# Quarter-array products for the odd groups, K^T V of two batches moved behind such products, K and V fetched ahead of Q, and the copies of the last column halves exchanged

## The chip, the cores and the metric

The kernel runs on one core of a Trainium2 chip. The metric is the device time of one execution in microseconds (us), lower is better. TensorE (PE in the profile, with its weight loads as PEld), VectorE (DVE), ScalarE (ACT) and GpSimd (POOL) compute; SyncE (SP), ScalarE and GpSimd issue transfers (DMA).

## The reference

For 8 batches, 8 heads, 576 rows and a head dimension of 64, attention without softmax, a normalisation for each head and row, and a feed-forward layer:

```python
kv = np.einsum('bhsd,bhse->bhde', k, v)
out = np.einsum('bhsd,bhde->bhse', q, kv)
rms = np.sqrt(np.mean(out * out, axis=-1, keepdims=True) + 1e-06)
out = out / rms * g_norm
x = out.transpose(0, 2, 1, 3).reshape(4608, 512)
h = x @ w_in                                    # 512 x 2048
g = np.where(h > 0.0, h, np.exp(np.minimum(h, 0.0)) - 1.0)
result = g @ w_out                              # 2048 x 512
```

The matrix products take bf16 operands and sum in float32.

## The kernel before

**Tokens.** A batch has 576 rows, held as 9 slots of 64. The 72 slots are taken eight at a time, so there are nine groups of 512 tokens (T = 0 to 8); `slot_of(T, n)` gives the batch and the slot. Since 9 is odd, each odd group (1, 3, 5, 7) has one pair of slots whose halves belong to two batches; in the even groups every pair is of one batch.

**Feed-forward.** A group's first product is eight steps `M0` to `M7`, each eight matmuls of 128x512 into a pair of PSUM banks (L381, `mm1_part`), followed by exp on ScalarE (L349) and two operations on VectorE that finish the elu (L361, L365; steps `E0` to `E7`). The second product is eight half-steps `H0` to `H7` of eight matmuls each (L402, `mm2_half`), whose results ScalarE copies out (L418).

**Attention of a group from 2 on.** `se_mm` (L240) multiplies the turned Q of two slots (128 tokens) by K^T V of their batch, for each of eight heads: contraction over 64, output 64 wide. Where both slots are of one batch, one matmul takes half of the array (64 rows, 128 columns; the profile writes 64\*128) and gives 128 tokens. Where they are of two batches, two matmuls take a quarter each (64\*64). A group is two calls, `se0` and `se1`. ScalarE squares (L276), VectorE sums (L282), ScalarE takes Ln and Exp (L290, L291), VectorE scales (L298), four DMA transposes turn the result (L305), VectorE multiplies by the gain (L311, steps `G0`, `G1`).

**K^T V of a batch** is `kv_all` (L257): 72 matmuls in quarters of the array (L155), 64x64 each, into a PSUM pair, and one copy by ScalarE (L261).

**The order** is written out by hand and no scheduler changes it. For each T from 2 to 8 `window` (L760) walks a string of steps: the first product of group T (M, E), the second of group T-1 (H), the attention of group T+1 (X: both products, squares, sums, inverse roots; Y: scale and transposes), and Q: turn Q of batch T+2 by DMA transposes on SP's queue (`turn_q`, L330), let GpSimd wait for them (`after_turn`, L338), and fetch batch T+3 (`fetch_ahead`, L92) by three transfers on GpSimd's queue: Q in float32, then K and V as bf16. GpSimd casts Q of batch T+2 at the start of window T (`cast_q`, L103). The letter after a step names its PSUM pair: A, B and C are one pair of banks each, and `o_ps` has the two banks left. Each is free again when its last reader is through. Window 2 has a string of its own, with `XB` in it; windows 3 to 7 go

```python
kv = f"K{T + 1}C" if T + 1 < B else ""
steps = (
    f"M0B {kv} H1 E0 M1A H3 E1 M2B H4 E2 H5 XA Y H6 Q M3B H7 E3 M4A E4 M5C E5 M6B G0 E6 M7A G1 E7 h0 h2"
)
```

so that K^T V of batches 4 to 7 stands in windows 3 to 6, between M0 and H1. The last 128 rows of the output are made in two halves of 256 columns (`last_columns`, L433): 16 matmuls of 128x256 each (L439), a copy (L110 on ScalarE, L112 on VectorE), and two transfers to memory, issued by ScalarE and SP (`last_store`, L426).

Of the kernel before, what the change touches and what calls it, by code (L numbers as in the profile page):

```python
# [8 lines left out]
FP32 = mybir.dt.float32  # L9
# [7 lines left out]
def kernel(  # L17
# [14 lines left out]
    P = 128  # L32

    B, H, S, D = q.shape
    DM = H * D
    DF = moe_w_in.shape[1]
    RK = S // 64
# [5 lines left out]
    V, A, Q = nc.vector, nc.scalar, nc.gpsimd  # L43

    const = ctx.enter_context(tc.tile_pool(name="const", bufs=1))
    stage = ctx.enter_context(tc.tile_pool(name="stage", bufs=1))
# [28 lines left out]
    def slot_of(T, n):  # L75
        return divmod(8 * T + n, RK)

    bf, raw = {}, {}
    src_of = {"q": q, "k": k, "v": v}

    def fetch(name, b, u=None):

        if (name, b) not in bf:
            bf[name, b] = qkvp.tile([P, 4, RK, D], BF16, name=f"{name}_bf", tag=name)
        ms = slice(0, 4) if u is None else slice(u, 4, 2)
        load(bf[name, b][:, ms], name, b, ms)

    def load(dst, name, b, ms=slice(0, 4), eng=nc.gpsimd):
        in_ = src_of[name][b].rearrange("h r d -> (h r d)").rearrange("(m p x) -> p m x", m=4, p=P)
        eng.dma_start(out=dst.rearrange("p m j d -> p m (j d)"), in_=in_[:, ms, :])  # L90

    def fetch_ahead(b):  # L92
        raw[b] = stage.tile([P, 4, RK, D], FP32, name="st_q", tag="q")
        load(raw[b], "q", b)
        for name in "kv":
            fetch(name, b)

    def cast_q(b):

# [67 lines left out]
    def kv_of(b, l, u, s):  # L167
        return kv_sb[l * 64 : l * 64 + 64, b, u, s]
# [46 lines left out]
    class Turned:  # L215
# [7 lines left out]
        def product(self, y):  # L223
            self.y = y
            y_mm(self.T, self.u, y)
# [11 lines left out]
        def scale(self, l):  # L237
            scale_t(self.T, self.y[l], self.r[:, l, :], 2 * l + self.u)

    def se_mm(T, h, se_ps):  # L240

        for i in range(2):
            (b0, j0), (b1, j1) = (slot_of(T, 4 * h + 2 * i + t) for t in range(2))
            parts = [(0, P, b0, j0, 2)] if b0 == b1 else [(0, 64, b0, j0, 1), (64, P, b1, j1, 1)]
            for m in range(4):
                u, s = m // 2, m % 2
                for l in range(2):
                    for lo, hi, b, j, n in parts:
                        nc.tensor.matmul(  # L249
                            se_ps[lo:hi, l, (4 * i + m) * 64 : (4 * i + m) * 64 + 64],  # L250
                            lhsT=qT[b][l * 64 : l * 64 + 64, s, u, j : j + n, :],
                            rhs=kv_of(b, l, u, s),
                            start=True,
                            stop=True,
                        )

    def kv_all(b, tag):  # L257
        kv_ps = pair(tag, "kv_ps")
        for u in range(2):
            kv_mm(b, [kv_ps[:, s, :] for s in range(2)], u)  # L260
        return lambda: nc.scalar.copy(  # L261
            kv_sb[:, b], kv_ps[:, :, 0:P].rearrange("p s (u e) -> p u s e", u=2)
        )

    def attention(T):

        st = {}

        def se(h):
            def product(tag="C"):  # L270
                st["se", h] = pair(tag, "se_ps")
                se_mm(T, h, st["se", h])

            def square():
                sq = attp.tile([P, 2, DM], BF16, name="sq", tag="sq")
                nc.scalar.activation(sq, st["se", h], AF.Square)  # L276
                st["sq", h] = sq

            def sums():
                ss = attp.tile([P, 2 * H], FP32, name="ss", tag="ss")  # L280
                st["ss", h] = ss
                nc.vector.reduce_sum(  # L282
                    out=ss,
                    in_=st.pop(("sq", h)).rearrange("p l (m e) -> p (l m) e", e=D),
                    axis=AX.X,
                )

            def inv():
                ss = st["ss", h]
                nc.scalar.activation(ss, ss, AF.Ln, bias=eps_col, scale=1.0 / D)  # L290
                nc.scalar.activation(ss, ss, AF.Exp, scale=-0.5)  # L291

            def scale():
                if h == 0:
                    st["xs"] = attp.tile([P, J, DM], BF16, name="xs", tag="xs")
                    x_tile(T)
                se_ps, ss = st.pop(("se", h)), st.pop(("ss", h))
                nc.vector.tensor_tensor(  # L298
                    out=st["xs"][:, 2 * h : 2 * h + 2, :].rearrange("p i (l m e) -> p l i m e", l=2, e=D),
                    in0=se_ps.rearrange("p l (i m e) -> p l i m e", i=2, e=D),  # L300
                    in1=ss.rearrange("p (l i m) -> p l i m", l=2, i=2).unsqueeze(4).to_broadcast([P, 2, 2, 4, D]),
                    op=ALU.mult,
                )
                for i in (2 * h, 2 * h + 1):
                    nc.sync.dma_start_transpose(  # L305
                        out=xT[T][:, :, i * P : i * P + P], in_=st["xs"][:, i, :]
                    )

            def gain():
                cols = slice(2 * h * P, 2 * h * P + 2 * P)  # L310
                nc.vector.tensor_scalar(  # L311
                    out=xT[T][:, :, cols],
                    in0=xT[T][:, :, cols],
                    scalar1=g_col,
                    scalar2=None,
                    op0=ALU.mult,
                )

            return product, square, sums, inv, scale, gain

        pieces = {}
        for h in range(2):
            for name, piece in zip(("se", "sq", "sum", "inv", "mul", "gain"), se(h)):
                pieces[f"{name}{h}"] = piece
        return pieces
# [106 lines left out]

    def last_columns():  # L433

        for n, eng in enumerate((A, V)):
            cols = slice(n * 256, n * 256 + 256)
            ps = single("m", "o_ps")[:, 0:256]
            for f in range(FC):
                nc.tensor.matmul(  # L439
                    ps,  # L440
                    lhsT=gT[NT - 1][:, f, (J - 1) * P : J * P],
                    rhs=w_out_sb[:, f, cols],
                    start=(f == 0),
                    stop=(f == FC - 1),
                )
            o = outp.tile([P, 2, DM], FP32, name="o_sb", tag="o")[:, 0, 0:256]
            copy_on(eng, o, ps)
            last_store(J - 1, o, cols)
# [93 lines left out]
    y_ps, sq0 = {}, {}  # L542
# [123 lines left out]
    for u in range(2):  # L666
        n = Turned(1, u)
# [92 lines left out]
    def window(T, steps):  # L760

        rest = {}
        nxt = attention(T + 1) if T + 1 < NT else None
        for step in steps.split():
            kind, arg = step[0], step[1:]
            if kind in "MR":  # L770
                i, tag = int(arg[0]), arg[1]
                make = mm1_rest if T == 2 and i == 0 else mm1
                rest[i] = make(T, i, tag, kind == "R")
            elif kind == "E":
                rest.pop(int(arg))()
            elif kind == "H":
                mm2_half(T - 1, int(arg))
            elif kind == "h":
                mm2_half(T, int(arg))
            elif kind == "K":  # L780
                kv_all(int(arg[0]), arg[1])()
            elif kind == "X":
                nxt["se0"](arg)
                nxt["se1"]("C")
                for name in ("sq0", "sq1", "sum0", "sum1", "inv0", "inv1"):
                    nxt[name]()
            elif step == "Y":
                nxt["mul0"]()
                nxt["mul1"]()
            elif step == "Q":  # L790
                b = T + 2
                if b < B:
                    turn_q(b)
                if b + 1 < B:
                    after_turn(b)
                    fetch_ahead(b + 1)
            elif kind == "G":
                nxt[f"gain{arg}"]()
            else:
                raise ValueError(step)  # L800
# [4 lines left out]
    for T in range(2, NT):  # L805
        if T + 2 < B:
            cast_q(T + 2)
        if T == 2:
            steps = "M0B K3C E0 M1A H5 E1 M2B E2 R3A H6 E3 XB Y H7 Q M4A E4 h0 R5B E5 M6C G0 E6 M7A G1 E7 h2"
        elif T + 1 < NT:  # L810
            kv = f"K{T + 1}C" if T + 1 < B else ""
            steps = (
                f"M0B {kv} H1 E0 M1A H3 E1 M2B H4 E2 H5 XA Y H6 Q M3B H7 E3 M4A E4 M5C E5 M6B G0 E6 M7A G1 E7 h0 h2"
            )
        else:
            steps = "M0B H1 E0 M1A H3 E1 M2B H4 E2 M3A H5 E3 M4B H6 E4 M5A H7 E5 M6B E6 M7A E7 h0 h2"
        window(T, steps)
# [33 lines left out]
```

## Time and profile before

| | |
|---|---|
| Median of 7 runs (lowest to highest) | 284.14 us (283.87 to 284.18) |
| The profiled execution: its own time | 284.04 us |
| Its span, first to last instruction | 282.3 us |
| PE busy | 273.8 us (97%) |
| DVE, ACT, POOL busy | 163.2, 141.6, 49.5 us |
| Granted TensorE clock | 1.0 |
| DMA | 39.46 MB, mean 140 GB/s |

Busy shares are averages over the whole span. The chain of work that ended last is more telling: it is followed backwards from the last instruction, at each step to what released it, and its pieces lie end to end, so that a piece which becomes shorter shortens the run unless another chain takes over. Matmuls are pipelined: 128x512 matmuls that follow each other start 0.216 us apart, though one lasts 0.38 us. Some records are missing from a trace: in the chain a group of eight such matmuls can appear as seven with a bit of "issue" in the place of the eighth; the distance between the starts of the pieces around it holds what it took.

### The profile page before, as it was taken

The numbers are of one execution on the slowest core, as the hardware profiler recorded it, in microseconds if no ns is written. First come the engines' busy times: TensorE is split into PE (matmuls) and PEld (weight loads), VectorE is DVE, ScalarE is ACT, GpSimd is POOL, SyncE is SP. The second block draws the span as 40 slices with busy tenths as digits, with TensorE's granted clock in tenths as the row PEclk, the third lists the DMA queues.
The fourth block names the chain that finished last, engine by engine and source line by source line (L and its number), as shares of the span: only waits on it lengthen the run. The fifth ranks groups of instructions, "written<-read, shape, count | busy, mean of one in ns | idle before, by whom it ended". The sixth has DMA issues, their size and how long they took to land.

```text
span 282.3 us, 5145 instructions
## 1 busy us (share of the span) xinstructions
PE 273.8 (97%) x2094; PEld 129.6 (46%) x2123; DVE 163.2 (58%) x222; ACT 141.6 (50%) x209; POOL 49.5 (18%) x89
## 2 busy tenths in 40 slices
PE   8899999999999999999999999999999999999994
PEld 3444444444544444444444444444444444444443
DVE  2549532967457746865587448834893489344600
ACT  3778359594566445533552445344543464333321
POOL 7743303322123033033003300000000000000000
PEclk9999999999999999999999999999999999999999
DMA  7999999899999969489438952612160215020222
GB/s 212 192 204 206 207 253 244 176 259 140 186 263 180 155 186 238 94 199 250 113 74 178 268 126 41 149 49 74 40 111 0 77 37 112 0 77 1 74 74 74
DMA packets 50571, 39.46 MB, mean 140 GB/s; under 512 B 30964, under 2 KB 44020, under 8 KB 50548
## 3 DMA queue, kind: packets, MB, share of 16 engines
q0 software_dynamic: 15008, 21.30, 37.7%
q1 hardware_dynamic: 35136, 17.31, 29.1%
q10 hardware_dynamic: 404, 0.53, 0.5%
q8 instruction: 16, 0.26, 0.4%
q14 instruction: 7, 0.06, 0.1%
HBM read 36.70 MB, written 9.44 MB: 163 GB/s over the span
## 4 chain that ended last, share of the span: by engine, by line
PE 95%; DVE 2%; issue 1%; ACT 1%; DVEq 0%
PE h_ps L381 42%; PE o_ps L402 42%; PE kv_ps L155 2%; PE se_ps L249 2%; PE kv_ps L524 2%; PE h_ps L568 1%; PE o_ps L439 1%; PE qt_ps L173 1%; PE mean L198 1%; DVE xT L211 1%; PE y_ps L188 1%; ACT elu_e L349 0%; DVE kv_sb L112 0%; ACT rT L631 0%; DVE qT L112 0%
## 5 line engine op out<-in xcount | busy, mean ns | idle before, releaser
L402 PE MATMUL o_ps<-w_out_sb,gT 128*128 128x512 bf16 x542 | 127.0, 379 | 1.5 <-issue 1.0
L381 PE MATMUL h_ps<-xT,w_in_sb 128*128 128x512 bf16 (+1 forms) x551 | 125.5, 376 | 0.6
L349 ACT ACTIVATE elu_e<-h_ps 128x1024 bf16<-128x1024 f32 (+1 forms) x79 | 74.0, 951 | 72.8 <-PE h_ps L381 71.5
L381 PEld LDWEIGHTS <-w_in_sb 128*128 128x128 bf16 x560 | 54.5, 98 | 64.4 <-issue 0.7
L402 PEld LDWEIGHTS <-gT 128*128 128x128 bf16 x560 | 53.5, 98 | 63.9 <-issue 0.9
L365 DVE TENSOR_TENSOR gT<-elu_e,h_ps 128x1024 bf16<-128x1024 bf16 (+1 forms) x67 | 77.2, 1157 | 6.9 <-DVE elu_e L361 0.5
L361 DVE TENSOR_SCALAR elu_e<-elu_e 128x1024 bf16<-128x1024 bf16 x72 | 31.6, 439 | 59.4 <-ACT elu_e L349 59.3
L418 ACT COPY o_sb<-o_ps 128x512 f32<-128x512 f32 x32 | 18.4, 588 | 31.0 <-PE o_ps L402 31.0
L103 POOL CAST q_bf<-st_q 128x384 bf16<-128x384 f32 x36 | 18.1, 549 | 40.2 <-DMA st_q<-in_q_dram 40.2
L282 DVE TENSOR_REDUCE ss<-sq 128x16 f32<-128x1024 bf16 x14 | 16.5, 1214 | 13.3 <-ACT sq L276 13.3
L298 DVE TENSOR_TENSOR xs<-se_ps,ss 128x1024 bf16<-128x1024 f32 x14 | 16.5, 1215 | 1.2 <-ACT ss L291 1.2
L276 ACT ACTIVATE sq<-se_ps 128x1024 bf16<-128x1024 f32 x14 | 13.7, 1029 | 0.3 <-PE se_ps L249 0.3
L211 DVE SCALAR_TENSOR_TENSOR xT<-y_ps,g_col,rT 128x512 bf16<-128x512 f32 (+1 forms) x10 | 6.2, 639 | 10.1 <-ACT rT L208 7.9
L338 POOL COPY gate<-qT 1x16 bf16<-1x16 bf16 x5 | 1.0, 193 | 55.9 <-DMA qT<-q_bf 55.9
L354 ACT ACTIVATE elu_h<-h_ps 128x1024 bf16<-128x1024 f32 (+1 forms) x12 | 9.3, 816 | 0.0
L90 POOL DMA_DIRECT2D v_bf<-in_v_dram x11 | 7.8, 712 | 4.1 <-DMA w_in_sb<-in_moe_w_in_dram 2.1
L155 PEld LDWEIGHTS <-k_bf 64*64 64x64 bf16 x576 | 6.3, 107 | 5.0 <-issue 4.6
L90 POOL DMA_DIRECT2D k_bf<-in_k_dram x11 | 7.7, 704 | 2.8 <-DMA w_in_sb<-in_moe_w_in_dram 2.1
L155 PE MATMUL kv_ps<-v_bf,k_bf 64*64 64x64 bf16 x576 | 7.5, 194 | 0.6 <-DVE kv_sb L112 0.4
L290 ACT ACTIVATE ss<-ss,eps_col 128x16 f32<-128x16 f32 x14 | 4.3, 308 | 6.4 <-DVE ss L282 6.4
L311 DVE TENSOR_SCALAR xT<-xT,g_col 128x1024 bf16<-128x1024 bf16 x14 | 6.7, 480 | 1.2 <-DMA xT<-xs 1.2
L365 DVE TENSOR_TENSOR gT<-elu_e,elu_h 128x1024 bf16<-128x1024 bf16 x9 | 6.3, 705 | 1.6 <-ACT elu_h L354 1.0
(56 smaller groups left out, 94.1 us busy)
## 6 DMA issues: line engine op xcount, KB each, us to landing
st_q<-in_q_dram POOLq DMA_DIRECT2D x6, 1152.0 KB, 8.2
out_dram<-o_sb SPq DMA_DIRECT2D x24, 256.0 KB, 3.3
k_bf<-in_k_dram POOLq DMA_DIRECT2D x6, 576.0 KB, 10.5
v_bf<-in_v_dram POOLq DMA_DIRECT2D x6, 576.0 KB, 13.0
out_dram<-o_sb SPq DMA_DIRECT2D x19, 128.0 KB, 2.4
w_out_sb<-in_moe_w_out_dram POOLq DMA_DIRECT2D x4, 512.0 KB, 15.6
w_in_sb<-in_moe_w_in_dram POOLq DMA_DIRECT2D x2, 512.0 KB, 10.9
q_bf<-in_q_dram POOLq DMA_DIRECT2D x3, 288.0 KB, 13.4
```

Of the source, the lines that this page charges most:

```text
L90: eng.dma_start(out=dst.rearrange("p m j d -> p m (j d)"), in_=in_[:, ms, :])
L103: nc.gpsimd.tensor_copy(out=bf["q", b][:, u, js], in_=raw[b][:, u::2, js, :].rearrange("p l j d -> p j l d"),)
L155: nc.tensor.matmul(kv_ps[s][l * 64 : l * 64 + 64, u * 64 : u * 64 + 64], lhsT=bf["k", b][rows, 2 * l + u, j, :], rhs=bf["v", b][rows, 2 * ...
L276: nc.scalar.activation(sq, st["se", h], AF.Square)
L282: nc.vector.reduce_sum(out=ss, in_=st.pop(("sq", h)).rearrange("p l (m e) -> p (l m) e", e=D), axis=AX.X,)
L298: nc.vector.tensor_tensor(out=st["xs"][:, 2 * h : 2 * h + 2, :].rearrange("p i (l m e) -> p l i m e", l=2, e=D), in0=se_ps.rearrange("p l ...
L349: nc.scalar.activation(e[:, lo:hi, :], h, AF.Exp)
L361: nc.vector.tensor_scalar(out=e, in0=e, scalar1=1.0, scalar2=1.0, op0=ALU.min, op1=ALU.subtract)
L365: nc.vector.tensor_tensor(out=gT[T][:, 2 * i + lo : 2 * i + hi, :], in0=e[:, lo:hi, :], in1=h, op=ALU.add if relu else ALU.max,)
L381: nc.tensor.matmul((ps[a] if isinstance(ps, list) else ps[:, a, :])[:, cols], lhsT=w_in_sb[:, c, f * P : f * P + P], rhs=xT[T][:, c, cols] ...
L402: nc.tensor.matmul(o_ps[T, j], lhsT=gT[T][:, f, j * P : j * P + P], rhs=w_out_sb[:, f, :], start=(f == 0), stop=(f == FC - 1),)
L418: nc.scalar.copy(o_sb[T, half][:, j % 2, :], o_ps[T, j])
```

## The change

Four parts. First, `se_mm` can make all its products in quarters; the step X asks for it where T is even (that is, for the odd groups 3, 5 and 7) and where K^T V follows (`XA6B` in window 4, for group 5, and `XA7B` in window 5, for group 6). Groups 4 and 8 stay as they were. Second, K^T V of batches 6 and 7 leaves windows 5 and 6 and goes into windows 4 and 5, directly behind `se1`, into the pair B; ScalarE's copy of it then stands between the two squares. Third, from window 3 on the fetch has K and V ahead of Q (batches 6 and 7). Fourth, VectorE copies the first half of the last columns and ScalarE the second.

```diff
-    def fetch_ahead(b):
-        raw[b] = stage.tile([P, 4, RK, D], FP32, name="st_q", tag="q")
-        load(raw[b], "q", b)
-        for name in "kv":
-            fetch(name, b)
+    def fetch_ahead(b, order="qkv"):
+        for name in order:
+            if name == "q":
+                raw[b] = stage.tile([P, 4, RK, D], FP32, name="st_q", tag="q")
+                load(raw[b], "q", b)
+            else:
+                fetch(name, b)
...
-    def se_mm(T, h, se_ps):
+    def se_mm(T, h, se_ps, quarters=False):
...
-            parts = [(0, P, b0, j0, 2)] if b0 == b1 else [(0, 64, b0, j0, 1), (64, P, b1, j1, 1)]
+            parts = [(0, 64, b0, j0, 1), (64, P, b1, j1, 1)]
+            if b0 == b1 and not quarters:
+                parts = [(0, P, b0, j0, 2)]
...
-        for n, eng in enumerate((A, V)):
+        for n, eng in enumerate((V, A)):
...
-                nxt["se0"](arg)
-                nxt["se1"]("C")
-                for name in ("sq0", "sq1", "sum0", "sum1", "inv0", "inv1"):
+                quarters = len(arg) > 1 or T % 2 == 0
+                nxt["se0"](arg[0], quarters)
+                nxt["se1"]("C", quarters)
+                nxt["sq0"]()
+                if len(arg) > 1:
+                    kv_all(int(arg[1]), arg[2])()
+                for name in ("sq1", "sum0", "sum1", "inv0", "inv1"):
                     nxt[name]()
...
-                    fetch_ahead(b + 1)
+                    fetch_ahead(b + 1, "qkv" if T == 2 else "kvq")
...
-            kv = f"K{T + 1}C" if T + 1 < B else ""
+            now = f"K{T + 1}C" if T in (3, 4) else ""
+            behind = f"{T + 2}B" if T in (4, 5) else ""
             steps = (
-                f"M0B {kv} H1 E0 M1A H3 E1 M2B H4 E2 H5 XA Y H6 Q M3B H7 E3 M4A E4 M5C E5 M6B G0 E6 M7A G1 E7 h0 h2"
+                f"M0B {now} H1 E0 M1A H3 E1 M2B H4 E2 H5 XA{behind} Y H6 Q M3B H7 E3 M4A E4 M5C E5 M6B G0 E6 M7A G1 E7 h0 h2"
             )
```

More of the change, by code (lines that the diff above doesn't have):

```diff
@@ L269, in se, with product @@
         def se(h):
-            def product(tag="C"):
+            def product(tag="C", quarters=False):
                 st["se", h] = pair(tag, "se_ps")
-                se_mm(T, h, st["se", h])
+                se_mm(T, h, st["se", h], quarters)
             def square():
```

## The prediction

> **What bounds the kernel now.** I read the page's first and fourth parts, then the chain of waits in order of time, then the timelines of single engines around the places that the diff touches.
>
> ```profile
> PE 273.8 (97%) x2094; PEld 129.6 (46%) x2123; DVE 163.2 (58%) x222; ACT 141.6 (50%) x209; POOL 49.5 (18%) x89
> PE 95%; DVE 2%; issue 1%; ACT 1%; DVEq 0%
> ```
>
> The chain is TensorE's own for 95% of the span: nothing else ends last for long, so what TensorE issues less is won, as long as no other engine becomes late. The chain of windows 4 to 6:
>
> ```profile
> 126.09 0.71 PE kv_ps L155 x72
> 126.79 0.16 issue
> 126.95 1.67 PE o_ps L402 x7
> 128.62 1.73 PE h_ps L381 x8
> ...
> 137.26 0.81 PE se_ps L249 x40
> 138.07 0.32 PE o_ps L402
> 138.39 0.05 issue
> 138.44 1.46 PE o_ps L402 x6
> 139.90 1.73 PE h_ps L381 x8
> ...
> 166.62 0.57 PE se_ps L249 x32
> ...
> 195.73 0.70 PE se_ps L249 x40
> ```
>
> Read the distance between the pieces of big matmuls on either side, less 1.73 us for the eight between (the piece of eight, 1.73, stands in the rows). K^T V costs 128.62 - 126.09 - 1.73 = 0.80, by the unrounded starts 0.81 us. The attention product of group 5 costs 139.90 - 137.26 - 1.73 = 0.91; group 3, worked out in the same way from its rows (82.00 to 84.64), 0.91; group 6 (166.62 to 169.02) 0.67; group 7 (195.73 to 198.27) 0.81; groups 4 and 8 0.68 each. The starts of the windows agree: 124.36, 153.72, 182.84, 212.08 and 240.39 give 29.36, 29.12, 29.24 and 28.31 us for windows 4 to 7; window 7, without K^T V, is 0.81 shorter than window 5, which has it. So an all-half product costs 0.68, and the same with one mixed pair 0.13 (pair at the end, one change of form more) or 0.23 (pair in the middle, two more): some 0.12 us for a change of form, of which the eight extra products are a part.
>
> ```profile
> 127.04 0.37 ACT L261 CAST kv_sb<-kv_ps 128x256 bf16<-128x256 f32 x1
> 135.43 1.22 DVE L365 TENSOR_TENSOR gT<-elu_e,h_ps 128x1024 bf16<-128x1024 bf16 x1
> 137.78 1.95 ACT L276 ACTIVATE sq<-se_ps 128x1024 bf16<-128x1024 f32 x2
> 155.37 0.78 PE L155 MATMUL kv_ps<-v_bf,k_bf 64*64 64x64 bf16 x72
> 276.71 0.37 ACT L110 COPY o_sb<-o_ps 128x256 f32<-128x256 f32 x1 [1.16 <-PE o_ps L439]
> 278.51 0.42 DVE L112 COPY o_sb<-o_ps 128x256 f32<-128x256 f32 x1 [11.10 <-PE o_ps L439]
> ```
>
> The fourth of these gives the price of a quarter product: 72 in 0.78 us, the last lasting 0.19, so (0.78 - 0.19)/71 = 8.3 ns from start to start. Four quarters work side by side.
>
> **The change, part by part.** *Price of a stretch of quarters.* 72 at 8.3 ns are 0.60; K^T V costs 0.81 in all, so entering and leaving the form costs 0.21. 64 products (an attention product in quarters) then cost 0.21 + 0.53 = 0.74, and 64 + 72 in one stretch 0.21 + 1.13 = 1.34 us.
>
> *Group 3 (window 2):* 0.91 becomes 0.74, -0.17. *Group 7 (window 6):* 0.81 becomes 0.74, -0.07. *Group 5 and K^T V of batch 6 (window 4):* 0.91 + 0.81 = 1.72 becomes 1.34, -0.38. *Group 6 and batch 7 (window 5):* 0.67 + 0.81 = 1.48 becomes 1.34, -0.14; here quarters make the product itself dearer by 0.07, and only the shared entry pays. Together -0.76 us.
>
> No trace of before has a stretch of 136 quarters or the passage from `se1` to K^T V. Bounds for that passage: nothing (both are quarters in the same places of the array; inside K^T V the passage from one column block to the other is not seen) and 0.12, a change of form. For a quarter product: 7.9 ns (the first sets of four inside K^T V start 31.6 ns apart) and 9.7 (0.70/72, ends included). I take nothing and 8.3, since rows of the very form give them. The dear ends cost 2 x 0.12 + 4 x 64 x 1.4 ns = 0.60; the cheap one gives 0.10.
>
> The Trainium skill speaks against the part: "TensorE: Matmul & The Clock Gate", section "Wait — 56ns, not 53.3ns?", has starts never closer than about 25 ns, however small the matmul. By it the 104 added products (24 + 24 + 32 + 24) would be 2.6 us, and after the saved switches the run some 1.6 us slower, an estimate from that page. The trace has 8.3 ns for such products in four quarters, so the row decides.
>
> *What the moved K^T V waits for.* It needs pair B, which M2B's elu leaves when DVE's operation at 135.43 ends, at 136.65; in window 4 it starts behind 64 products, near 137.7: 1 us spare. It needs K and V of batch 6 by then. Their transfers:
>
> ```profile
> st_q<-in_q_dram POOLq DMA_DIRECT2D x1, 1152.0 KB, 8.6
> k_bf<-in_k_dram POOLq DMA_DIRECT2D x1, 576.0 KB, 11.1
> v_bf<-in_v_dram POOLq DMA_DIRECT2D x1, 576.0 KB, 13.6
> ```
>
> Issued at 122.68, 123.43 and 124.16, they land at 131.3, 134.5 and 137.8, one behind the other: in the old order V would be there 0.1 us before its use. With K and V first, V lands near 133 and Q last, near 137.8. GpSimd's casts of Q (2.96 us, at 131.38 now) then end near 140.8; behind them on POOL wait the gate at 151.3 and the next fetch. SP turns batch 6 at 147.59, behind the transposes of xs, so 6 us are spare. In window 5 the transfers land by 165.9, K and V near 161, for K^T V near 166.6; the casts end near 169, SP's turn is at 178. The casts move onto DVE's sums and scales; in window 2 they lie there already (85.15 to 87.9) and those took their usual 1.21 us. Cost nothing.
>
> *ScalarE.* The copy (0.37) goes between the squares. Queued behind it are the second square and what hangs on it: DVE's second sum starts 0.2 later (it stands in DVE's queue behind the first sum, which hides the rest), the scales follow 0.2 to 0.35 later, while TensorE's own stretch is longer by 1.34 - 0.91 = 0.43. M4A, which waits for the first scale, has 1.0 us spare now (142.3 against 143.36) and keeps it. M3B, which now waits for the copy: the copy ends near 139.3, M3B starts behind H6 near 140.4. 1.1 us spare; if that cover went, M3B to M7A would start later by what is missing. Transposes and gains keep their 1.6 us before the next M0, for the same reason.
>
> *Windows 5 and 6 without K^T V at their start* are ordered as window 7 is now, and its chain has no wait there. H1's gT has the 16 matmuls of h0 and h2 and M0 as cover.
>
> *The end.* The last copy is on the path. VectorE starts it 0.09 after the last matmul's end and takes 0.42; ScalarE, in the first half, 0.04 and 0.37. That is -0.10; between -0.05 (the durations alone) and -0.15. ScalarE now issues the first half's transfer before that copy (0.50 us, from about 277.2), through at 277.7, well before 278.4. SP's queue keeps its order.
>
> **Sum:** -0.76 - 0.10 = -0.86 us on the profiled execution's 284.04 (span 282.3 and 1.7 around it): 283.18. The median lies 0.10 above that execution, so 283.25, -0.3%. Measurement can tell about 0.2% (0.57 us) from nothing: a limit of 283.57.
>
> **Rivals.** *1. The saving is half as large:* the passage costs a switch, or a long stretch runs at the dear price. Against: the rows of the form. 0.86 - 0.60 gives -0.26, so 283.5 to 283.9. *2. The won time is handed on:* a wait of about 1 us more than its cover in windows 4 and 5 (the copy before M3B, or pair B). For: spare times are only 1.0 to 1.2. Against: each was counted along its queue. Half a us lost twice gives about 284.2. *3. The instruction stream, slower than before.* The long stretch is 136 pairs of weight load and matmul, 272 instructions in 1.13 us; the longest now is 144. The page's instruction queue brought 16 blocks, 0.26 MB, in 0.4% of 16 engines' time, so about 1.1 us for a block of 16 KB. If a block runs out inside each long stretch and the next is a whole 1.1 us away, the two cost 2.2 - 0.86 = +1.3, 285.5; it decides from 0.72 us a stretch. Against: K^T V now eats 144 instructions in 0.6 us with no gap. No row shows how far ahead TensorE holds instructions. "Runtime: NRT & Kernel Launch", section "Instruction fetch mechanics", of the Trainium skill gives TensorE room for 2048 instructions and in another sentence two lines of 256; the first excludes this rival, the second doesn't.
>
> **How the numbers follow.** Forecast (283.0 to 283.45) 0.66; rival 1, 0.14, about a third of it under the limit; rival 2, 0.10, mostly within 0.2%, a fifth slower; rival 3, 0.10. Faster 0.66 + 0.05 = 0.71; slower 0.02 + 0.08 = 0.10, the short stalls of rival 3 being no change; the same 0.19. The range 282.95 to 284.0 holds the forecast, rival 1 and part of rival 2.
>
> **What would show it.** In the profile after: one se stretch directly followed by 72 kv products in windows 4 and 5 with no idle time between, 1.34 us in all; window 2 shorter by 0.17, window 4 29.79, window 5 28.98, window 6 28.36; no chain piece of ACT or DVE in windows 4 and 5; the last transfer issued 0.7 us behind the last matmul's start. A gap inside the stretch is rival 3, one before M3B rival 2; starts further apart than 8.3 ns rival 1.

## The result and the profile after

The changed kernel takes 283.3 us (median of 15 runs, 283.18 to 284.12) against 284.11 before (35 runs): a ratio of 0.9975, with a 95% interval of 0.9968 to 0.9982. That is 0.81 us less; the forecast was 283.25. The profiled execution took 283.27 us, its span is 281.5 us (before 284.04 and 282.3).

The page of the changed kernel, part one and, of part three, the queue that brings instructions:

```profile
PE 272.3 (97%) x2198; PEld 129.2 (46%) x2227; DVE 163.0 (58%) x222; ACT 142.0 (50%) x209; POOL 49.1 (17%) x89
...
q8 instruction: 17, 0.28, 0.4%
```

There are 104 matmuls more, and TensorE is busy 1.5 us less. Of these, 0.98 lie in the first 12.5 us (10.42 before, 9.44 after), where TensorE waits for data and the change does nothing; what was won has to be read from the chain. There TensorE's share goes from 95% to 92%, because in this execution its first part runs through a transfer of V (4.96 to 12.08 us); window 2's product of group 3 still starts at 81.98, against 82.00 before. The chain of waits of the changed kernel around the places of the change, with the starts of windows 4, 5 and 6 at 124.17, 154.00 and 183.03:

```profile
81.98 0.64 PE se_ps L254 x64
...
84.45 1.73 PE h_ps L386 x8
...
124.17 1.73 PE h_ps L386 x8
...
137.07 0.64 PE se_ps L254 x64
137.71 0.65 PE kv_ps L157 x72
138.36 0.32 PE o_ps L407
138.68 0.05 issue
138.73 1.46 PE o_ps L407 x6
140.19 1.73 PE h_ps L386 x8
...
154.00 1.73 PE h_ps L386 x8
...
166.09 0.64 PE se_ps L254 x64
166.73 0.66 PE kv_ps L157 x72
...
169.22 1.73 PE h_ps L386 x8
...
183.03 1.73 PE h_ps L386 x8
...
195.12 0.64 PE se_ps L254 x64
...
197.59 1.73 PE h_ps L386 x8
```

In windows 4 and 5 each attention product runs into K^T V with no piece between, and no piece of another engine stands in the chain of these windows. Read as before, less 1.73 us for the eight big matmuls: 140.19 - 137.07 - 1.73 = 1.39 in window 4, 169.22 - 166.09 - 1.73 = 1.40 in window 5. Alone in quarters the products of groups 3 and 7 cost 0.74 each (81.98 to 84.45, 195.12 to 197.59). Window 6 ends at 211.40.

| us | before | forecast | after |
|---|---|---|---|
| group 3, product | 0.91 | 0.74 | 0.74 |
| group 5 and K^T V of batch 6 | 1.72 | 1.34 | 1.39 |
| group 6 and K^T V of batch 7 | 1.48 | 1.34 | 1.40 |
| group 7, product | 0.81 | 0.74 | 0.74 |
| window 4 | 29.36 | 29.79 | 29.83 |
| window 5 | 29.12 | 28.98 | 29.03 |
| window 6 | 29.24 | 28.36 | 28.37 |

The products together: 4.92 became 4.27, -0.65. The end, in the timeline of ScalarE and its queue, changed kernel:

```profile
274.90 2.14 ACTq L431 DMA_DIRECT2D out_dram<-o_sb  x2
277.77 0.37 ACT L112 COPY o_sb<-o_ps 128x256 f32<-128x256 f32 x1 [2.91 <-PE o_ps L444]
278.18 0.50 ACTq L431 DMA_DIRECT2D out_dram<-o_sb  x1
```

The first half's transfer is issued behind VectorE's copy, among the two that end at 277.04; ScalarE's copy of the second half ends at 278.14 and the transfer follows. From the start of the last matmul to SP's last transfer it is 0.71 us now and was 0.82.

### The profile page after: what moved, and what is told of

Read it like the earlier page. It is cut to its first block, busy times and chain, and to the rows that moved or that the text cites. A ratio compares the mean times of both kernels' runs of the same rounds, so it can differ in the third digit from the quotient of the medians.

```text
span 281.5 us, 5354 instructions
## 1 busy us (share of the span) xinstructions
PE 272.3 (97%) x2198; PEld 129.2 (46%) x2227; DVE 163.0 (58%) x222; ACT 142.0 (50%) x209; POOL 49.1 (17%) x89
## 3 DMA queue, kind: packets, MB, share of 16 engines
HBM read 36.70 MB, written 9.44 MB: 164 GB/s over the span
## 4 chain that ended last, share of the span: by engine, by line
PE 92%; DMA 3%; POOL 1%; issue 1%; ACT 1%; DVE 1%; POOLq 0%
PE h_ps L386 42%; PE o_ps L407 42%; DMA v_bf<-in_v_dram 3%; PE kv_ps L157 2%; PE se_ps L254 2%; PE h_ps L573 1%; PE o_ps L444 1%; POOL k_bf L90 1%; PE mean L200 0%; PE qt_ps L175 0%; PE y_ps L190 0%; POOL v_bf L90 0%; ACT elu_e L354 0%; DVE xT L213 0%; POOL q_bf L90 0%
```

## The experiments

All kernels below were run beside the kernel before on the same chip. Differences of 0.1 us are smaller than the spread of the times, so the verdicts rest on lengths in the chain, which agree to 0.01 us from run to run; only the first microseconds, in which TensorE waits for data, differ by up to 0.5.

### Quarters alone

```diff
-            parts = [(0, P, b0, j0, 2)] if b0 == b1 else [(0, 64, b0, j0, 1), (64, P, b1, j1, 1)]
+            parts = [(0, 64, b0, j0, 1), (64, P, b1, j1, 1)]
+            if b0 == b1 and T == 2:
+                parts = [(0, P, b0, j0, 2)]
```

> The kernel before, with the attention products of groups 3 to 8 all in quarters and nothing else changed: K^T V stays at the start of windows 3 to 6. If the price is 0.21 us for entering and leaving the form and 8.3 ns for a quarter product, every attention product costs 0.74: groups 3 and 5 fall from 0.91 by 0.17 each, group 7 from 0.81 by 0.07, groups 4, 6 and 8 rise from 0.68 by 0.06 each. Sum -0.23 us, so 283.9. If what counts is the shared entry alone, and quarters do nothing by themselves, groups 3, 5 and 7 stay at 0.91 and 0.81 and the time at 284.1.

Median 283.95 us, ratio 0.9995 (0.9985 to 1.0004): by the time alone not to be told from no change, and -0.2 was all that was expected. The chain decides. Group 5 in this kernel (the rows of group 5's product and what follows it):

```profile
137.19 0.64 PE se_ps L251 x64
...
139.67 1.73 PE h_ps L383 x8
```

139.67 - 137.19 - 1.73 = 0.75. The same for all six groups, 0.75 each by the unrounded starts: groups 3 and 5 fell by 0.17, group 7 by 0.06, groups 4, 6 and 8 rose by 0.07. So the price of the form holds, and quarters pay only where a mixed pair had forced changes of form.

### K^T V behind products that are not in quarters

```diff
-                quarters = len(arg) > 1 or T % 2 == 0
+                quarters = False
```

> The changed kernel with the old forms of the attention products: halves, and quarters for the mixed pairs alone. K^T V of batches 6 and 7 still stands behind them. By the prices, against the changed kernel: group 5 with K^T V, three changes of form inside, 1.64 instead of 1.39 (window 4 longer by 0.25); group 6 with K^T V, one change inside, 1.40 instead of 1.39 (window 5 the same); group 3 longer by 0.17, group 7 by 0.07. In all 283.8. If the form has to be the same for the entry to be shared, group 6 with K^T V costs 0.67 + 0.81 = 1.48 and window 5 is longer by 0.09.

> The kernel of the run behind_no_quarters once more, for a profile at the full clock (the first one's fell to 0.56). The same numbers are expected: window 4 longer than in the changed kernel by 0.25, window 5 the same if a change of form inside a shared stretch costs 0.12 and no more (1.40), longer by 0.09 if the entry is not shared (1.48); group 3 at 0.91, group 7 at 0.81; time 283.8.

The median of the first run is 283.76 us, ratio 0.9986 (0.9977 to 0.9996). The chain read here is that of the second (one run, 283.96 us):

```profile
137.49 0.81 PE se_ps L254 x40
138.30 0.71 PE kv_ps L157 x72
...
140.84 1.73 PE h_ps L386 x8
...
166.74 0.57 PE se_ps L254 x32
167.31 0.71 PE kv_ps L157 x72
...
169.85 1.73 PE h_ps L386 x8
```

Window 4: 140.84 - 137.49 - 1.73 = 1.62 (1.64 expected, 1.39 in the changed kernel). Window 5: 1.38, against 1.40 in the changed kernel and 1.48 for the two apart. So what is saved in window 5 comes from the place of K^T V alone: a stretch that begins in halves and ends in quarters is as short, and the quarters of group 6 bring nothing. In window 4, of the 0.33 saved, the quarters bring 0.23, by the two changes of form that the mixed pair had cost, and the place of K^T V the other 0.10.

### Q fetched first again

```diff
-                    fetch_ahead(b + 1, "qkv" if T == 2 else "kvq")
+                    fetch_ahead(b + 1, "qkv")
```

> The changed kernel, with Q fetched ahead of K and V again for batches 6 and 7. If the new order is needed: V of batch 6 lands near 137.7, TensorE would begin K^T V behind the 64 products at 137.55, so it waits 0.1 to 0.4 us in window 4; in window 5 V lands near 165.9, 0.7 before its use, and nothing waits. Time 283.4 to 283.7. If the order is idle: the window 4 of the changed kernel, 29.83, and 283.3.

The time is 283.5 us, ratio 0.9978 (0.9969 to 0.9987), the span 281.5. The issues of batch 6 in this run, size and time to landing:

```profile
st_q<-in_q_dram POOLq DMA_DIRECT2D x1, 1152.0 KB, 9.3
k_bf<-in_k_dram POOLq DMA_DIRECT2D x1, 576.0 KB, 10.8
v_bf<-in_v_dram POOLq DMA_DIRECT2D x1, 576.0 KB, 13.1
```

V, issued at 124.02, landed at 137.1; K^T V started at 137.61, with no idle time before it. The long stretch cost 1.40 and window 4 was 29.83 long, as in the changed kernel. The expected wait did not come: the new order was not needed in this execution, which at 283.27 us is among the fastest of the ten. The median is 0.2 above that of the changed kernel and lies in the range that was expected if the order is needed; whether the slower executions waited for V is not shown. The order moves the landing from 0.5 before the use to 3 us before it (in the changed kernel V is issued at 123.28 and lands 11.2 later, at 134.5), a margin, and in the execution read no time.

### The last two copies alone

```diff
-        for n, eng in enumerate((A, V)):
+        for n, eng in enumerate((V, A)):
```

> The kernel before, with the engines of the last two copies exchanged and nothing else. From the start of the last matmul to SP's last transfer 0.71 us instead of 0.82, and all behind it earlier by 0.11: 284.0. If the two transfers that ScalarE issues get into each other's way, 0.82 or more and 284.1 or more.

283.9 us, ratio 0.9999 (0.999 to 1.0008): the time cannot show 0.1. From the last matmul's start SP's last transfer was issued 0.71 us later, and the program ended 4.00 later; before, 0.82 and 4.12. In SP's queue the last three stores are nearer together, from

```profile
275.57 3.85 SPq L426 DMA_DIRECT2D out_dram<-o_sb  x3
```

before (start, then length from the first issue to the end of the last) to this in the run:

```profile
275.73 3.75 SPq L426 DMA_DIRECT2D out_dram<-o_sb  x3
```

### The passage without a third wait

```diff
-            behind = f"{T + 2}B" if T in (4, 5) else ""
+            behind = f"{T + 2}C" if T in (4, 5) else ""
...
+            if behind:
+                steps = steps.replace("M3B", "M3C").replace("M5C", "M5B").replace("M6B", "M6C")
...
-                nxt["se1"]("C", quarters)
+                nxt["se1"]("B" if len(arg) > 1 else "C", quarters)
```

> The changed kernel, with the second attention product of groups 5 and 6 in pair B and K^T V in pair C (M3, M5 and M6 of windows 4 and 5 exchange B and C accordingly). The passage to K^T V in the changed kernel holds a gap of 0.06 us and, in the weight loads' queue, one instruction of 51 ns that only waits: the first pair of K^T V has three waits (K, V, pair B), and two find room on the weight load and the matmul. In pair C the third is already covered by a wait before. If that instruction is the gap, the long stretch falls from 1.39 to 1.34 us in windows 4 and 5: -0.10, 283.2. If the gap belongs to the passage, it stays at 1.39.

283.48 us, ratio 0.9974 (0.9964 to 0.9984). The instruction that only waits is gone from the trace, and the longest distance between two starts in the stretch fell from 61 to 43 ns. But the chain says:

```profile
137.57 0.64 PE se_ps L254 x64
138.21 0.65 PE kv_ps L157 x72
...
140.70 1.73 PE h_ps L386 x8
```

140.70 - 137.57 - 1.73 = 1.40, as with the gap. The reason that I had given for the missing 0.05 us falls: the gap is absorbed, the stretch is no shorter without it. From the first start to the last, 136 products take 1.167 us in both kernels, 8.6 ns each, where 72 take 0.581 (8.2) and 64 take 0.524 (8.3). What makes the second half of a long stretch dearer stays open. It needs no passage and no change of kind: in the run with sixteen repeats below, behind the first gap one set of four products of K^T V follows the other after about 32 ns at first, and after 33 to 34 ns from about the fortieth product on.

### One stretch of 208 products

```diff
-            now = f"K{T + 1}C" if T in (3, 4) else ""
+            now = f"K{T + 1}C" if T == 3 else ""
...
+                copies = []
+                if T == 4:
+                    copies.append(kv_all(5, "B"))
+                    copies.pop()()
                 nxt["se0"](arg[0], quarters)
+                if T == 4:
+                    copies.append(kv_all(6, "C"))
...
```

> As the run with exchanged pairs, and K^T V of batch 5 leaves the start of window 4 as well: K^T V of 5, first attention product, K^T V of 6, second attention product, 208 products in one stretch. If entering and leaving the form is what is paid for, 0.21 once more is saved: the stretch costs 0.21 + 208 x 8.35 ns = 1.95, window 4 is 27.6 + 1.95 = 29.6 long instead of 29.83, and the time 283.0. ScalarE's copy for batch 5 has about 0.2 us to spare before the second product. If TensorE's instruction stream (rival 3) limits long stretches, 416 instructions in a row show gaps and the window does not become shorter.

283.2 us (283.07 to 283.34), ratio 0.9968 (0.9955 to 0.998). The chain of window 4:

```profile
124.31 1.73 PE h_ps L386 x8
...
136.40 0.71 PE kv_ps L157 x72
137.11 0.27 PE se_ps L254 x32
137.37 0.65 PE kv_ps L157 x72
138.02 0.27 PE se_ps L254 x32
138.29 0.16 issue
138.45 1.67 PE o_ps L407 x7
140.12 1.73 PE h_ps L386 x8
...
153.94 1.73 PE h_ps L386 x8
```

The stretch costs 140.12 - 136.40 - 1.73 = 1.99 (1.95 expected), window 4 is 29.63 long (29.83 in the changed kernel): 0.20 saved, one more way in and out. By the chain this is the shortest kernel of the study; by the times it is not separated from the changed one.

### The same stretch at another place in the instruction stream

```diff
-    idle(10, kv_ps[:, 0, :])
+    idle(4, kv_ps[:, 0, :])
+    for _ in range(78):
+        nc.tensor.matmul(kv_ps[0:32, 0, 0:16], lhsT=zeros[0:32, 0:32], rhs=zeros[0:32, 0:16], start=True, stop=True)
```

> The run one_stretch with 144 more instructions on TensorE long before, in the time in which it waits for the first Q (six idle matmuls are exchanged for 78 tiny ones), so that the stretch of 208 products lies differently against the blocks of 256 instructions. In the run with 16 repeats the first gap came 173 products after the start of the stretch, and the next ones each 128 products, 256 instructions, later; counted in the program the gaps lie at 247 above a multiple of 256, and one_stretch begins its stretch at 249, this kernel at 137. If blocks are what made the gaps, this stretch now breaks near its 183rd product, with a gap of 0.5 to 2 us, and window 4 is longer by as much than 29.63. If only a stretch of many blocks can break, it costs 2.00 as before.

287.65 us (one run). Some 2.2 us of this are lost in the first 20, where TensorE's products now last longer (the second sixteen turns of Q 0.99 us instead of 0.57); group 3's product starts 2.2 later. TensorE in window 4, from the timeline:

```profile
138.53 0.78 PE L157 MATMUL kv_ps<-v_bf,k_bf 64*64 64x64 bf16 x72
139.12 0.45 PE L254 MATMUL se_ps<-kv_sb,qT 64*64 64x64 bf16 x32
139.40 0.66 PE L157 MATMUL kv_ps<-v_bf,k_bf 64*64 64x64 bf16 x52
142.13 0.35 PE L157 MATMUL kv_ps<-v_bf,k_bf 64*64 64x64 bf16 x20 [2.07 <-issue]
142.31 0.43 PE L254 MATMUL se_ps<-kv_sb,qT 64*64 64x64 bf16 x32
```

The stretch breaks behind 72 + 32 + 52 = 156 products, with 2.07 us in which TensorE waits for nothing that the profile shows. The stretch and the window are those of the unbroken one; what differs is the count of instructions before them. I had placed the break at the 183rd product, counting 173 products to the first gap in the run with sixteen repeats. That run's trace, below, has 64 + 82 = 146. The difference is 54 instructions, so the gaps lie at 193 above a multiple of 256, not at 247; from this stretch's start at 137 that is 56 and then 56 + 256 = 312 instructions, 156 products, where it broke. So the count of blocks of 256 instructions gives the place of the break: the first boundary, after 56 instructions, passed without a gap, and the second did not. The unshifted stretch, from 249 on, meets only one, after 200 instructions.

### K^T V sixteen times over

```diff
-        for u in range(2):
-            kv_mm(b, [kv_ps[:, s, :] for s in range(2)], u)
+        for _ in range(16 if b == 7 else 1):
+            for u in range(2):
+                kv_mm(b, [kv_ps[:, s, :] for s in range(2)], u)
```

> The changed kernel with the 72 products of K^T V of batch 7 issued 16 times over (the same values): 64 + 1152 quarter products in a row in window 5, 2432 instructions. If TensorE is supplied with instructions as fast as it issues them, the stretch is 15 x 72 x 8.35 ns = 9.0 us longer and the time 292.3, with starts 8.3 ns apart throughout. If only a few hundred instructions are held and a block of 256 takes 1.1 us or more, the spacing is the same at first and then breaks: a gap of about a us for each block, 293 to 301.

316.64 us (one run). TensorE in window 5, from the timeline:

```profile
166.84 0.86 PE L157 MATMUL kv_ps<-v_bf,k_bf 64*64 64x64 bf16 x82
167.92 1.24 PE L157 MATMUL kv_ps<-v_bf,k_bf 64*64 64x64 bf16 x128 [0.22 <-issue]
171.93 1.92 PE L157 MATMUL kv_ps<-v_bf,k_bf 64*64 64x64 bf16 x128 [2.76 <-issue]
175.65 1.93 PE L157 MATMUL kv_ps<-v_bf,k_bf 64*64 64x64 bf16 x128 [1.81 <-issue]
```

From its first product's start to its last one's the stretch takes 32.92 us instead of 1.17, 31.8 more and not 9.0. The first gap, of 0.22 us, comes behind 64 + 82 = 146 products; from there on the gaps come every 128 products, that is 256 instructions, and are 1.8 to 2.8 us long. This is the block of 16 KB that the instruction queue brings: with 2160 instructions more than the changed kernel the page has 26 packets where that has 17.

```profile
q8 instruction: 26, 0.43, 0.5%
```

One block takes 3.7 to 4.0 us from start to start. The granted clock falls in the stretch, and with it 128 products last 1.92 us instead of the 1.24 of the first block; that the idle time lowers the clock fits this run but is not tested, and the single gap of 2.07 us in the shifted stretch left the clock at 1.00:

```profile
160.00:166.00 6.00, 5.95 (x29) 2.65 (x28) 3.30 (x4) 2.09 (x3) 0.00 (x0) 1.00 1.05 332
166.00:200.00 34.00, 17.78 (x1219) 15.99 (x1219) 1.22 (x1) 2.06 (x4) 2.76 (x6) 0.58 0.03 8
```

(Window, its length, busy time and instructions of PE, PEld, DVE, ACT and POOL, the granted clock, DMA share and GB/s: the clock is 1.00 before the stretch and 0.58 on average in it.)

### The copy later

```diff
                 if len(arg) > 1:
-                    kv_all(int(arg[1]), arg[2])()
+                    copy = kv_all(int(arg[1]), arg[2])
                 for name in ("sq1", "sum0", "sum1", "inv0", "inv1"):
                     nxt[name]()
+                    if len(arg) > 1 and name == ("inv1" if T == 4 else "sq1"):
+                        copy()
```

> The changed kernel, with ScalarE's copy of K^T V later: in window 4 behind both inverse roots, in window 5 behind the second square. This takes the spare time of M3B, which needs the pair that the copy reads. Window 4: the copy ends near 141.7, M3B could start at 140.2, so a wait of about 1.5 us appears before it and window 4 grows by as much. Window 5: the copy ends 0.2 before M3B could start, no wait, window 5 as in the changed kernel. Time 284.8. If M3B does not depend on the copy in time, both windows stay and the time is 283.3.

285.25 us (one run). Windows 4 and 5 are 31.70 and 29.03 long. ScalarE and TensorE of window 4, from their timelines:

```profile
141.60 0.35 ACT L266 CAST kv_sb<-kv_ps 128x256 bf16<-128x256 f32 x1
142.01 1.89 PE L386 MATMUL h_ps<-xT,w_in_sb 128*128 128x512 bf16 x8 [1.71 <-ACT kv_sb L266]
```

M3B waits 1.71 us for the copy, and the window grows by 1.87. In window 5, where the copy ends at 170.79 and M3B could start a little later than 171.0, nothing waits. So M3B depends on the copy, and the spare time was about one microsecond.

## Why the prediction was right

**What bounds the kernel.** TensorE's chain. Of 0.65 us that its products became shorter, and 0.11 at the end, the median shows 0.81: nothing was handed on to another engine. That the median came within 0.05 us of the forecast is partly luck: the chain gave 0.10 less than forecast, and the median of the changed kernel lies 0.03 above its profiled execution and not the 0.10 that was added.

**Price of a stretch.** 0.21 for the way in and out and 8.3 ns for a product. Confirmed by eight attention products in quarters with no K^T V behind them (0.74 to 0.75, 0.74 forecast) and by one entry more saved in the stretch of 208 (0.20). The long stretches cost 1.39 and 1.40 instead of 1.34: the term "64 + 72 at 8.3 ns" was too small by 0.05 us each, 8.6 ns is what they measured. The passage that I had bounded by 0 and 0.12 had a gap of 61 ns, but without that gap the stretch was as long, as the exchange of the pairs shows.

**Parts.** Group 3 -0.17 and group 7 -0.07 as forecast; group 5 with batch 6 -0.33 (forecast -0.38); group 6 with batch 7 -0.08 (-0.14); the end -0.11 (-0.10). Sum -0.76 against -0.86.

**Waits.** The copy before M3B: the changed kernel ends the two copies at 138.88 and 167.91, M3B starts near 140.0 and 169.1, so 1.1 us were spare as counted, and the late copy shows the dependence. Pair B was free in time: VectorE's operation ends at 136.46, K^T V starts near 137.6. The order of the fetch I had said to cost nothing, and in window 4 it cost nothing; but the readings under it were off: in the old order V comes 0.5 us before its use and not 0.1, and in the new one it lands at 134.5 and not near 133.

**Rivals.** Of the first (a saving smaller by 0.60) a sixth came, the 0.05 us in each long stretch; its sign, starts further apart than 8.3 ns, was there. The second (time handed on) did not come. The third has a real mechanism, and I had it too cheap and too far away: a block that is missing cost 1.8 to 2.8 us but for the first gap of 0.22, and not 1.1, and stretches broke after 156 and 146 products, where the changed kernel's have 136. It did not come because 136 were short enough at both of their places. In the shifted run the stretch of window 5 stands 144 instructions further on and did not break either (170.47 to 173.60, so 1.40 again). By the count of blocks its 272 instructions would meet a second boundary only where the first lies within their first 16; no run has such a place.

**The skill against the rows.** "TensorE: Matmul & The Clock Gate", section "Wait — 56ns, not 53.3ns?", has a floor of about 25 ns between starts. The trace has 8.3 to 8.6 ns for products in four quarters, and following the page the change would have been forecast slower. "Runtime: NRT & Kernel Launch", section "Instruction fetch mechanics", gives TensorE room for 2048 instructions; the runs broke after 312 and 292 instructions of the stretch, so the measurement is nearer to the other sentence of the page, which has two lines; of 256 instructions each, these hold 512.

## What to carry to other kernels

Where small products stand between big ones, read the cost of a stretch from the starts of the big matmuls around it and split it into a way in and out and a price for each product: here the way costs as much as 25 products. Putting two stretches together saved 0.10 to 0.21 us, and taking out the changes of form that a mixed pair forces 0.06 to 0.23; where nothing forces a change, quarters made a product 0.07 dearer. A stretch of some hundred and fifty products can outrun the supply of instructions; count two instructions for each, and keep it short. And a moved step is best costed with the spare time of every wait beside it, since the same copy, moved behind the inverse roots, cost 1.9 us.

## What the runs showed that I had not expected

TensorE can run out of instructions: 256 of them took 3.7 to 4.0 us to come in a long row of small products, and where a stretch stands against the blocks decided whether 208 products cost 1.99 us or 2.25 more. A gap of 61 ns inside the long stretch cost nothing. And the granted clock averaged 0.58 over a stretch in which TensorE had some 2 us of idle time in each 4.
